# Earlier first tile, gated casts and a new order of visits in a fused attention and MLP kernel

## The chip, the cores and the metric

The kernel runs on one core of a Trainium2 chip. Times are device microseconds of one execution. The time before was 373.53 us, the median of 4 runs (372.5 to 373.75). The profiled run of the kernel before is a fifth one, and it took 374.65 us. The profiled executions had a mean granted TensorE clock of 0.993 to 1.000. The "span" is the time from the first to the last instruction in the profile; it is about 2 us shorter than the device time.

## The reference, cut to what matters

```python
# q, k, v: [8, 12, 448, 64] float32; w_in: [768, 2048]; w_out: [2048, 768]
scores = q @ k.T / sqrt(64) - log(448)        # per batch and head
attn   = 1 / (1 + exp(-scores))               # a sigmoid, no softmax
x      = (attn @ v), heads side by side       # [3584, 768]
h      = x @ w_in
out    = (h * sigmoid(h)) @ w_out             # [3584, 768] float32
```

Below, FF1 is the product with w_in and FF2 the product with w_out. A "bank" is a part of PSUM, the memory that TensorE writes to, and an "eviction" is the copy out of it.

## The kernel before: the parts that matter

A batch is three quads of four heads. TensorE runs through everything in one fixed order: attention of the next batch (the "visits", each of one to three units, a unit being a score step with its sigmoid, or the value product of a quad) is woven into the MLP of the batch before it. FF1 of batch 0 is 96 plain matmuls; later FF1 and FF2 stages multiply sums of blocks, and VectorE makes those sums.

The head: VectorE and ScalarE warm up, k of quad 0 comes as float32 and is cast by VectorE, everything else of the first two batches comes by GpSimd's casting loads (DMAs that turn float32 into float16 on the way).

```python
nc.vector.memset(bias_s, NEG_LOG_S)
nc.scalar.activation(warm[:, 0:1], bias_s, AF.Sigmoid, bias=bias_s, scale=1.0)
nc.vector.memset(warm, 0.0)               # waits for the activation
...
load32(1, 0)                              # k, quad 0, two DMAs on one queue
load16(0, 0)                              # q, quad 0, casting load by GpSimd
make_identity(nc, ident)
...                                       # VectorE casts k in two parts
load16(1, 1); load16(0, 1); load16(1, 2); load16(0, 2); load16(2, 0)
dummy(12)                                 # warm TensorE up on zeros
... # transposes of quad 0, then the first scores
behind = [
    [L(1, 3), L(0, 3), T(1, 1, 2)],       # loads of quad 3, transposes of quad 1
    ...
    [T(0, 2, 3), L(1, 5), L(0, 5), L(2, 2), W(0), W(1)],   # w_in pieces 0 and 1
    [], [T(1, 3, 2)], [T(0, 3, 3)],       # transposes of quad 3
    ...
    [V(2, 2, 3, 4), F(4)],                # first 4 matmuls of FF1, batch 0
```

Later quads are fetched as float32 and cast by GpSimd, then transposed by DMA:

```python
def prepare(i):
    for t in (1, 0):
        cast(t, i)                        # GpSimd, into st16[t]
        dma_transpose(t, i)
for i in range(NQ + 1, B * NQ - 2):
    at(("s", i, 3), lambda j=i + 2: prepare(j))
```

The end of a FF2 stage on VectorE is: eviction of the last value product to xT, four subtractions of 0.27 us (`x_sums`), the last two evictions of FF2, then sums of gT for the next FF2 (`g_sums`).

## Time and profile before

| | before |
|---|---|
| time, median of 4 | 373.53 us |
| span of the profiled run (374.65 us) | 372.9 us |
| TensorE busy, idle | 358.4 us, 14.5 us |
| first score | 9.18 us |
| first FF1 matmul of batch 0 | 29.70 us |
| FF1 of batch 1, 2, 3 starts | 60.75, 107.95, 153.04 us |

The rows from "first score" down are starts of TensorE's instructions in the timeline. The difference between two of them is the length of a stage. The prediction below shows the lines themselves.

### The profile page before, as it was taken

To read this page: it belongs to the slowest core of one execution; us is meant where nothing else is said; L and a number is where in the kernel's file an instruction comes from. 1 tells how busy PE (TensorE), PEld (TensorE's weight loads), DVE (VectorE), ACT (ScalarE), POOL (GpSimd) and SP (SyncE) were. 2 spreads that over 40 slices of the span, in tenths; PEclk is the share of its full clock that TensorE was granted. 3 is DMA by queue.
4 is the path that set the end of the run, shared out by engine and by line. 5 is a ranking of instruction groups with operands and counts; after the bars stand their busy time and mean duration, and the time that the engine had idled before them with its cause. 6 is when DMAs were issued, how large, how long until landed. Compare 5 with 4: busy or idle time off the path is not lost.

```text
span 372.9 us, 8674 instructions
## 1 busy us (share of the span) xinstructions
PE 358.4 (96%) x3598; PEld 238.9 (64%) x3598; DVE 229.9 (62%) x385; ACT 255.0 (68%) x290; POOL 161.1 (43%) x162
## 2 busy tenths in 40 slices
PE   6988999999999999999999999999999999999995
PEld 2553446964469755796548955598447965489652
DVE  2762698859775665755746656527368657436762
ACT  2998885777746788467884688657994679846100
POOL 8962230394322933249222691228733491006500
PEclk9999999999999999999999999999999999999999
DMA  8999999759889099760997629964697925130133
GB/s 145 183 185 205 229 227 178 125 121 140 154 191 205 2 148 202 165 179 9 180 200 139 164 46 192 190 152 114 76 191 152 195 44 115 38 86 3 42 86 84
DMA packets 64071, 51.13 MB, mean 137 GB/s; under 512 B 36768, under 2 KB 60576, under 8 KB 64032
## 3 DMA queue, kind: packets, MB, share of 16 engines
q1 hardware_dynamic: 48464, 35.86, 44.7%
q0 software_dynamic: 15328, 14.32, 25.6%
q8 instruction: 28, 0.46, 0.5%
q10 hardware_dynamic: 240, 0.39, 0.3%
q14 instruction: 11, 0.09, 0.1%
HBM read 45.61 MB, written 11.01 MB: 152 GB/s over the span
## 4 chain that ended last, share of the span: by engine, by line
PE 82%; DVE 7%; ACT 5%; DMA 3%; issue 1%; POOL 1%; ACTq 0%; DVEq 0%
PE ffp L465 34%; PE att L343 23%; PE att L172 8%; PE att L188 7%; PE ffp L343 7%; ACT attnT L178 4%; DMA w_in_sb<-in_moe_w_in_dram 3%; PE ffp L87 1%; DVE xT L206 1%; DVE w_out_sb L424 1%; DVE xT L218 1%; PE att L275 1%; PE ffp L275 1%; DVE sw L311 1%; DVE sw L310 1%
## 5 line engine op out<-in xcount | busy, mean ns | idle before, releaser
L178 ACT ACTIVATE attnT<-att,bias_s 128x896 f16<-128x896 f32 x168 | 156.8, 1013 | 26.7 <-PE att L172 23.6
L364 POOL TENSOR_TENSOR gT<-attnT,gT 128x896 f16<-128x896 f32 x42 | 77.9, 1885 | 65.5 <-ACT gT L362 65.5
L126 POOL CAST st<-st 128x896 f16<-128x896 f32 x36 | 35.0, 987 | 107.9 <-DMA st<-in_k_dram 95.3
L343 PEld LDWEIGHTS <-w_in_sb 128*128 128x128 f16 x672 | 64.4, 98 | 1.8 <-issue 1.1
L374 ACT COPY attnT<-att 128x896 f32<-128x896 f32 x35 | 31.7, 905 | 45.9 <-PE att L343 45.9
L343 PE MATMUL att<-xT,w_in_sb 128*128 128x224 f16 x588 | 61.1, 259 | 0.5 <-DVE xT L206 0.5
L465 PEld LDWEIGHTS <-gT 128*128 128x128 f16 x416 | 39.3, 98 | 29.2 <-issue 5.6
L465 PEld LDWEIGHTS <-gs 128*128 128x128 f16 x384 | 34.7, 98 | 31.9 <-issue 11.7
L465 PE MATMUL ffp<-w_out_sb,gT 128*128 128x384 f16 x288 | 51.3, 326 | 0.0
L343 PEld LDWEIGHTS <-sw 128*128 128x128 f16 x504 | 48.3, 98 | 1.4 <-issue 1.4
L362 ACT ACTIVATE gT<-attnT 128x896 f16<-128x896 f32 x42 | 39.9, 951 | 11.7 <-DVE attnT L378 10.9
L172 PE MATMUL att<-qkT,qkT 64*64 64x448 f16 x588 | 42.0, 359 | 2.6 <-ACT attnT L178 1.0
L378 DVE TENSOR_TENSOR attnT<-att,attnT 128x896 f32<-128x896 f32 x28 | 30.6, 1091 | 21.4 <-PE att L343 19.9
L206 DVE TENSOR_SCALAR xT<-att 128x896 f16<-128x896 f32 x22 | 24.0, 1090 | 27.6 <-PE att L188 24.5
L465 PE MATMUL ffp<-wt,gs 128*128 128x384 f16 x192 | 36.3, 327 | 0.0
L465 PE MATMUL ffp<-w_out_sb,gs 128*128 128x384 f16 x192 | 36.1, 327 | 0.0
L476 DVE TENSOR_SCALAR snap<-ffp 128x384 f32<-128x384 f32 x40 | 22.2, 554 | 22.3 <-PE ffp L465 22.2
L343 PE MATMUL att<-xT,sw 128*128 128x224 f16 x336 | 35.6, 259 | 0.0
L188 PE MATMUL att<-attnT,v 64*64 64x448 f16 x588 | 32.8, 352 | 0.0
L172 PEld LDWEIGHTS <-qkT 64*64 64x64 f16 x588 | 17.3, 105 | 24.2 <-issue 17.6
L479 DVE SCALAR_TENSOR_TENSOR osb<-ffp,snap 128x384 f32<-128x384 f32 x40 | 22.1, 554 | 15.3 <-PE ffp L465 15.0
L378 DVE TENSOR_TENSOR attnT<-ffp,attnT 128x448 f32<-128x448 f32 x28 | 16.1, 616 | 19.7 <-PE ffp L343 19.7
(71 smaller groups left out, 343.6 us busy)
## 6 DMA issues: line engine op xcount, KB each, us to landing
out_dram<-osb SPq DMA_DIRECT2D x53, 192.0 KB, 3.1
st<-in_k_dram SPq DMA_DIRECT2D x38, 224.0 KB, 4.5
st<-in_q_dram SPq DMA_DIRECT2D x36, 224.0 KB, 4.9
v<-in_v_dram POOLq DMA_DIRECT2D x44, 112.0 KB, 4.3
w_in_sb<-in_moe_w_in_dram POOLq DMA_DIRECT2D x4, 768.0 KB, 14.9
w_out_sb<-in_moe_w_out_dram POOLq DMA_DIRECT2D x4, 768.0 KB, 20.2
sw<-in_k_dram POOLq DMA_DIRECT2D x8, 112.0 KB, 4.5
sw<-in_q_dram POOLq DMA_DIRECT2D x8, 112.0 KB, 4.6
```

The lines of the kernel that those rows point to most:

```text
L126: nc.gpsimd.tensor_copy(st16[kind].rearrange("p r e d -> p e r d"), st32[kind].rearrange("p e (r d) -> p e r d", r=R),)
L172: nc.tensor.matmul(att[pair][cj, e, :S], kT[re, r, cj], qT[re, :, cj], start=True, stop=True)
L178: nc.scalar.activation(attnT[:, s0 : s0 + 2, :], att[pair][:, :, :S], AF.Sigmoid, bias=bias_s, scale=QKSCALE)
L188: nc.tensor.matmul(bank(pair, j)[e * HP : (e + 1) * HP, :S], vt[rj, e, r, :], attnT[rj, s0 + e, :], start=(r == 0), stop=(r == R - 1),)
L206: nc.vector.tensor_scalar_mul(x, att[pair][:, :, :S], SX)
L343: nc.tensor.matmul(o, a[:, c, (4 * s + f) * P : (4 * s + f + 1) * P], xb[:, c], start=first and c == 0 and f % 2 == 0, stop=c == KC - 1, s ...
L362: nc.scalar.activation(oo, ap, AF.Sigmoid, bias=0.0, scale=ISX)
L364: nc.gpsimd.tensor_mul(oo, ap, oo)
L374: nc.scalar.copy(as2(h[:, i, c], ap), ap)
L378: nc.vector.tensor_add(as2(h[:, i, c], ap), ap, as2(h[:, i, c], ap))
L465: nc.tensor.matmul(bank, a[:, fc], w[:, fc], start=first and fc == 0, stop=fc == KH - 1, skip_group_check=True,)
L476: nc.vector.tensor_scalar_mul(snap[i], bank, ISX)
```

## The change

Its intent: start TensorE's warm-up and the first scores earlier; keep GpSimd's casts apart in time from the sums that VectorE makes on the way to the next FF1; and place the visits of batch 1 better between the FF1 steps of batch 0.

```diff
+    nc.vector.memset(warm, 0.0)
     nc.vector.memset(bias_s, NEG_LOG_S)
-    nc.scalar.activation(warm[:, 0:1], bias_s, AF.Sigmoid, bias=bias_s, scale=1.0)
-    nc.vector.memset(warm, 0.0)
...
-    load32(1, 0)
+    for lo, hi in ((0, 4), (4, R)):
+        c = slice(lo * D, hi * D)
+        for g, queue in enumerate((nc.sync, nc.scalar)):
+            queue.dma_start(st32[1][g * HP : (g + 1) * HP, :, c], src_of(1, 0, g)[:, :, c])
     load16(0, 0)
+    nc.scalar.activation(start_s, bias_s, AF.Sigmoid, bias=bias_s, scale=1.0)
...
-    dummy(12)
+    dummy(10)
...
-        (8, "v", 0), (17, "v", 0), (26, "v", 0), (32, "w", 0), (35, "v", 0), ...
+        (8, "v", 0), (21, "v", 0), (24, "w", 0), (30, "v", 0), (35, "v", 0), ...
...
-        at(("s", i, 3), lambda j=i + 2: prepare(j))
+        if i % NQ < NQ - 1:
+            at(("s", i, 3), lambda j=i + 2: prepare(j))
...
         if parts[0][1] == 2:
             g_sums(parts[0][0], 4)
+        if b + 1 < B:
+            for t in range(2):
+                nc.vector.memset(st16[t][:, 0, 0, 0:1], 0.0)
+            prepare(b * NQ + NQ + 1)
         ff1(b, ((1, 3), (2, 0)))
```

Below, "the head" is the first part of this, "the new order" the list of visits, and "the gate" the memsets with the moved `prepare`: the cast must wait for a one-element write that stands behind the sums in VectorE's order.

## The prediction

> **What bounds the kernel now.** I read the page first, then the list of waits, then the timelines of the three places that the change touches. The page says that TensorE is the bound almost everywhere:
> ```profile
> PE 358.4 (96%) x3598; PEld 238.9 (64%) x3598; DVE 229.9 (62%) x385; ACT 255.0 (68%) x290; POOL 161.1 (43%) x162
> ```
> The reader is to see how little there is to win: the span is 372.9 us, so TensorE idles 14.5 us in all. 2% is 7.5 us. The table of stretches of 10 us puts the idle time in few places: 3.3 us in the first 10 us, 1.1 and 1.9 us in the next two, about 0.5 to 0.7 us each in the stretches from 50, 60, 80, 100 and 150 us, and 4.5 us at the end, which the change does not touch. The waits say what ended those gaps:
> ```profile
> PE ffp L275 <- DMA w_in_sb<-in_moe_w_in_dram: 1.1, 1, 1.1
> PE ffp L343 <- DVE osb L529: 1.1, 2, 0.6
> ```
> The first is a wait for the first piece of w_in at 29.7 us, the second two equal waits of 0.56 us at the starts of the second and third FF1 stage (109.8 and 154.9 us). Now the head, TensorE alone:
> ```profile
> 2.77 4.96 PE L87 MATMUL ffp<-warm 128*128 128x512 f16 x12 [2.77 <-DVE warm L80]
> 7.67 0.41 PE L148 MATMUL att<-ident,st 128*64 128x128 f16 x8
> 7.91 0.56 PE L148 MATMUL ffp<-ident,st 128*64 128x128 f16 x14
> 8.30 0.33 PE L148 MATMUL att<-ident,st 128*64 128x128 f16 x6
> 9.18 0.38 PE L172 MATMUL att<-qkT,qkT 64*64 64x448 f16 x4 [0.55 <-ACT qkT L158]
> ```
> Twelve dummies start late (VectorE's memset of `warm` waited for ScalarE's warm-up activation, which writes a column of it) and end at 7.7 us, although the k tile was in and cast before that; VectorE's own timeline has its cast behind the last landing of k:
> ```profile
> 6.53 0.69 DVE L569 CAST st<-st 128x512 f16<-128x512 f32 x2 [3.81 <-DMA st<-in_k_dram]
> ```
> So the head looks like 1 to 2 us of free gain. But GpSimd issues the casting loads of the next quads back to back, each pair in about 1.2 us, from 1.25 us until w_in:
> ```profile
> 9.08 1.25 POOL L119 DMA_DIRECT2D st<-in_k_dram  x2
> 10.32 1.20 POOL L119 DMA_DIRECT2D st<-in_q_dram  x2
> ```
> These are k and q of quad 3. The DMA views of 5 to 10 us and of 10 to 15 us give their time to landing (last column, us):
> ```profile
> st<-in_k_dram POOLq DMA_DIRECT2D x2, 112.0 KB, 4.6
> ```
> ```profile
> st<-in_q_dram POOLq DMA_DIRECT2D x2, 112.0 KB, 4.5
> ```
> The second DMA of each pair is issued half a pair later, so quad 3's k is complete at 9.08 + 0.62 + 4.6 = 14.3 us and its q at 10.32 + 0.60 + 4.5 = 15.4 us. TensorE uses them here:
> ```profile
> 14.62 0.58 PE L148 MATMUL att<-ident,st 128*64 128x128 f16 x14
> 15.20 0.38 PE L172 MATMUL att<-qkT,qkT 64*64 64x448 f16 x4
> 15.52 0.58 PE L148 MATMUL ffp<-ident,st 128*64 128x128 f16 x14
> ```
> So the kernel runs only 0.3 and 0.1 us behind its loads at 15 us. And the chain that ended last does not go through the dummies after that; it goes through GpSimd's issues and this load:
> ```profile
> 19.19 10.46 DMA w_in_sb<-in_moe_w_in_dram
> ```
> The first w_in piece lands at 29.65 us, and FF1 of batch 0 cannot start before, whatever ScalarE and TensorE have finished. DMA is 9 tenths busy from the first landing to 70 us.
>
> The third place is the end of a batch's last visits, all engines:
> ```profile
> 107.65 0.27 DVE L218 TENSOR_TENSOR xT<-xT 128x224 f16<-128x224 f16 x1
> 107.66 1.05 POOL L126 CAST st<-st 128x896 f16<-128x896 f32 x1 [7.04 <-DMA st<-in_k_dram]
> ...
> 107.83 1.00 DVE L218 TENSOR_TENSOR xT<-xT,xT 128x224 f16<-128x224 f16 x1
> ```
> The same subtraction takes 0.27 us alone and 1.00 us when GpSimd's cast of the prefetched k tile runs. What follows on VectorE (the last two evictions of FF2, L479 and L529) ends 0.73 us later, and TensorE waits 0.56 us for the bank that L529 frees. The next sum (L446) also goes from 0.69 to 1.35 us under the cast of q, but nothing waits for it then.
>
> **What the skill says.** The Trainium skill, "SBUF — State Buffer", section "Who interferes with whom": a VectorE instruction with two SBUF inputs contends with a GpSimd instruction that reads SBUF, and the one that starts first blocks the other until it is done. The trace agrees: the sum at 107.83 us ends just after the cast (108.71 us), and the 0.73 us added is most of one cast. "DMA: Bandwidth & Descriptors", section "Issuing engines are not separate DMA queues": several issuing engines save only the sequencer's issue time, since all DMAs share the same 16 engines. Here the two k issues took 1.43 us on one queue, so the saving can be about 0.7 us. "TensorE: Matmul & The Clock Gate", section "What's actually happening": the array runs at half clock until it has been busy for some 3.4 us. The trace shows dummies starting 0.43 us apart until about 7 us and 0.2 us for the last two, so ten dummies should warm it up, or nearly.
>
> **The change, part by part.**
>
> *Head.* Removed: the wait of `warm` for the activation (1.6 us) and two dummies. The memset comes first on VectorE, at about 0.8 us for 0.27 us, so the dummies start at about 1.15 us and ten of them at 0.43 us end at 5.4 us in place of 7.7 us. k in four parts on two queues: the first parts of both halves are issued at 0.73 us together; before, the first issued DMA had the 4.2 us median to landing, and 256 KB now come where 224 KB came, so they should be in at about 4.5 to 5 us, the rest at about 6. ScalarE has the table load and its activation behind two issues, done near 4 us, before it is wanted. The q tile still comes by GpSimd, issued at 1.25 and 1.9 us with a similar 4.1 us or more in a busy stretch, so at about 6.1 to 6.7 us; its transposes and the two copies (0.35 and 0.3 us) give a first score at about 7.7 us in place of 9.18: **1.5 us earlier**. On the path to the end: almost none. Scores stay ahead only until the transposes of quad 3, which cannot move before 14.3 and 15.4 us; there 0.1 to 0.3 us of the 1.5 are left. What is left runs into w_in at 29.65 us: GpSimd's order is unchanged, its only idle time before the issue is 0.21 us (L119 at 11.73 us), so w_in lands at most 0.2 us earlier. I book **0.1 us**.
>
> *Gated casts.* The memsets of one element of `st16` stand in VectorE's order behind the x sums (and the g sums where FF2 starts with a pair), the casts behind them. Added: two memsets of about 0.06 us for each of six batches, beside TensorE. Moved: casts and DMA transposes some 1 to 4 us later, into a FF1 stage of about 15 us; the tiles are first scored some 10 us after that stage, so nothing should wait for them. Removed: 0.56 us at the second and 0.56 us at the third FF1 stage, the two waits listed: **1.1 us**. The other FF1 starts show no wait. The cast under the long sum of w_out at 84 us (3.88 us for two, 1.82 elsewhere; then 0.71 us of TensorE waiting) belongs to a quad whose prepare is not moved, so that wait stays.
>
> *Visits of batch 1 moved.* The same work in another order between 30 and 62 us. TensorE's visible waits there are 0.32 us (56.0), 0.35 us (59.3) and 0.54 us (62.2); and score groups of eight that take 0.49 us when fed are stretched to about 0.8 us at 36.7 and 39.3 and 0.7 us at 46.9: about 0.8 us. Sum: some 2 us at most. ScalarE is almost as full (8.9 of 10 us from 30 to 50). The new order has 13 steps before the second visit, which takes away the stretch at 36.7, spreads the w sums out, and takes the long in-place sum out of the way of the last eviction to xT. Against it: visits only 5 and 4 steps (1.0 and 0.8 us) apart, where two sigmoids need 1.9 us, and two steps between the last two visits. I book **0.4 us**.
>
> Sum: 0.1 + 1.1 + 0.4 = 1.6 us; 373.5 - 1.6 = **371.9 us**.
>
> **Rivals.** (a) The head counts in full: 1.5 us more, 370.4 us. For it: the dummies stand on the chain. Against it: loads at 14.3, 15.4 and 29.65 us that do not move. It would need w_in to land earlier. (b) The casts merely hit other VectorE work in FF1, or the late transposes hold up a score: the 1.1 us are lost or halved, about 372.6 us. Against it: VectorE has idle stretches there, and its work on PSUM has only one SBUF input. (c) The new order of visits is worse: ScalarE piles up between the close visits and TensorE loses 0.5 to 1 us, giving about 373 us. (d) The new order takes most of its 2 us: 370.3 us.
>
> **Range and chances.** Each term has about its own size as its error: head 0 to 0.7 (1.5 in the rival), casts 0.5 to 1.4, order -0.7 to 1.5. Combined, 0.2 to 3.2 us, and the runs before spread over 1.1 us. Range 370.3 to 373.3 us. Over 2% would need 7.5 us, half of all idle time; slower by 2% would need a new wait in every batch. Faster 0.02, same 0.97, slower 0.01.
>
> **What would show each step.** Right: first score near 7.7 us, but the quad 3 transposes at 14.3 and 15.4 us or later, a wait for w_in grown to about 2 us, FF1 of batch 0 still starting at 29.4 to 29.8 us; no L218 of 1.00 us, no waits of L343 for L529; the 0.71 us wait near 88 us still there. Wrong: FF1 of batch 0 starting over 0.7 us earlier, a wait of a score for a transposed tile, or TensorE idling more from 30 to 62 us than its 1.4 us of before.

## The result, and the profile after

The changed kernel took 374.87 us (median of 4, 374.31 to 375.48) against 373.53 us for the kernel before. The ratio is 1.0042, with a 95% interval of 1.0017 to 1.0066. Ratios are the mean time of one kernel's fast runs over that of the other's of the same rounds, so they are not quite the ratio of the medians; nor quite that of the means over all rounds that I quote below, from which they differ by up to 0.0010. Later rounds, told below, put the same two kernels at 0.9990 to 0.9998.

The page of the changed kernel has almost the same TensorE line; busy time says nothing here:

```profile
PE 358.9 (96%) x3596; PEld 239.2 (64%) x3596; DVE 224.0 (60%) x397; ACT 255.6 (69%) x290; POOL 160.0 (43%) x162
```

The list of TensorE's waits (total us, times, longest us) does say something:

```profile
PE ffp L148 <- DMA st<-in_q_dram: 2.5, 2, 2.0
PE att L172 <- ACT attnT L178: 1.7, 5, 0.5
PE ffp L87 <- DVE bias_s L80: 1.2, 1, 1.2
```

The waits for w_in (1.1 us) and for the evicted bank (1.1 us in two) are gone from the list. In their place stands one wait of 2.0 us for a q tile. TensorE's timeline of the head shows it (start us, us busy, then the wait in brackets):

```profile
1.19 4.45 PE L87 MATMUL ffp<-warm 128*128 128x512 f16 x10 [1.19 <-DVE bias_s L80]
5.57 0.64 PE L148 MATMUL att<-ident,st 128*64 128x128 f16 x8
6.62 0.83 PE L148 MATMUL ffp<-ident,st 128*64 128x128 f16 x14 [0.42 <-DMA st<-in_q_dram]
...
8.14 0.38 PE L172 MATMUL att<-qkT,qkT 64*64 64x448 f16 x4 [0.52 <-DVE qkT L158]
...
14.31 0.58 PE L148 MATMUL att<-ident,st 128*64 128x128 f16 x14 [0.17 <-DMA st<-in_k_dram]
...
17.24 0.83 PE L148 MATMUL ffp<-ident,st 128*64 128x128 f16 x14 [2.03 <-DMA st<-in_q_dram]
...
30.73 0.93 PE L275 MATMUL ffp<-xT,w_in_sb 128*128 128x448 f16 x4
```

The first score comes 1.04 us earlier than before. At 14.31 us, k of quad 3 leaves 0.3 us of that. Then q of quad 3, used at 15.52 us before, holds TensorE until 17.24 us. FF1 of batch 0 starts at 30.73 us, 1.03 us later than before, and this time it waits for no w_in.

The third reading is the end of the second FF2 stage:

```profile
108.70 0.27 DVE L218 TENSOR_TENSOR xT<-xT,xT 128x224 f16<-128x224 f16 x1
...
109.36 0.55 DVE L529 TENSOR_SCALAR osb<-ffp 128x384 f32<-128x384 f32 x1
...
109.97 1.31 PE L343 MATMUL ffp<-xT,sw 128*128 128x224 f16 x12
...
112.39 0.07 DVE L709 MEMSET st<- 128x1 f16 x2
...
112.60 1.81 POOL L126 CAST st<-st 128x896 f16<-128x896 f32 x2 [11.72 <-DVE st L709]
```

The fourth sum takes 0.27 us in place of 1.00, the second product of FF1 (109.97 us) waits for nothing, and the casts run behind the memsets. The stage from FF1 of batch 2 to FF1 of batch 3 is 44.38 us (108.82 to 153.20) in place of 45.09. So one part did what it should, and something else gave more back.

### The profile page after: what moved, and what is told of

Same layout as the page of the kernel before. It is cut to its first block, busy times and chain, and to the rows that moved or that the text cites. A ratio compares the mean times of both kernels' runs of the same rounds, so it can differ in the third digit from the quotient of the medians.

```text
span 373.1 us, 8705 instructions
## 1 busy us (share of the span) xinstructions
PE 358.9 (96%) x3596; PEld 239.2 (64%) x3596; DVE 224.0 (60%) x397; ACT 255.6 (69%) x290; POOL 160.0 (43%) x162
## 5 line engine op out<-in xcount | busy, mean ns | idle before, releaser
L126 POOL CAST st<-st 128x896 f16<-128x896 f32 x36 | 34.1, 967 | 118.6 <-DMA st<-in_k_dram 52.0
L362 ACT ACTIVATE gT<-attnT 128x896 f16<-128x896 f32 x42 | 39.9, 951 | 11.6 <-DVE attnT L378 10.9
L188 PE MATMUL att<-attnT,v 64*64 64x448 f16 x588 | 33.7, 359 | 0.0
```

The lines of the kernel that those rows point to most:

```text
L126: nc.gpsimd.tensor_copy(st16[kind].rearrange("p r e d -> p e r d"), st32[kind].rearrange("p e (r d) -> p e r d", r=R),)
L188: nc.tensor.matmul(bank(pair, j)[e * HP : (e + 1) * HP, :S], vt[rj, e, r, :], attnT[rj, s0 + e, :], start=(r == 0), stop=(r == R - 1),)
L362: nc.scalar.activation(oo, ap, AF.Sigmoid, bias=0.0, scale=ISX)
```

## The experiments

Each was run with five rounds (six runs, profiled one included) unless said otherwise. Rounds ran in four sessions: chip 2, chip 0 twice (these two share eleven runs of the kernel before), chip 9.

### First session: one part at a time

**The kernel before against itself.** No edit.

> The kernel before, unchanged, against itself: ratio 1.000 with an interval of some 0.2%. It also gives a second trace. If the loss of the change is real, its trace again has no wait of TensorE for the q tile of quad 3 (about 15.4 us), FF1 of batch 1 starting at 60 to 61 us, and the span is below the changed kernel's by the 0.3% or so that the times differ by. If instead the first profile of before was a lucky or unlucky sample, the start of FF1 of batch 1 moves by 1 us or more between the two traces of the same kernel.

Measured: 374.55 us mean (373.14 to 376.67), ratio 0.9999, interval 0.9965 to 1.0033. The seventeen runs of the kernel before on this chip spread from 372.73 to 376.67 us. The three timed runs that I had before the prediction spread over 1.1 us; with the profiled run (374.65 us), which I also had and left out, it is 2.15 us. So a single kernel moves by 4 us from one execution to the next, and one trace shows one draw. In its second trace FF1 of batch 1 started at 60.88 us (60.75 in the first), q of quad 3 was transposed at 16.45 us in place of 15.52, and only one of the two waits for the bank was there.

**The head alone.**

```diff
 # the memset, load, activation and dummy(10) hunks of the change; nothing else
```

> Before plus the head part alone (early memset, k in four parts on two queues, late table warm-up, ten dummies). Theory A, the head does the harm: TensorE runs early into the loads of quad 3, sits over 1 us on them, its clock is granted at less than full afterwards (the changed kernel's trace has 2.03 us and a granted clock of 0.87 from 10 to 20 us), and the time is 1.5 to 2.5 us above before (ratio 1.004 to 1.007). Theory B, the order of visits does it: the head alone is within 0.3 us of before (ratio 0.999 to 1.001) or a little faster.

Measured: 375.08 us mean against 374.52, ratio 1.0013, interval 0.9985 to 1.0041: no gain, and no loss that stands clear of the spread. Its list of waits:

```profile
PE ffp L465 <- DVE snap L476: 1.8, 1, 1.8
PE ffp L275 <- DMA w_in_sb<-in_moe_w_in_dram: 1.5, 1, 1.5
```

The first score came at 7.71 us, 1.5 us earlier than in the first trace of before, and FF1 of batch 0 waited 1.5 us for w_in and started at 29.94 us. That is the head's gain ending in a wait for a load. Theory A and theory B both fall as put: neither part costs 1.5 us by itself. The wait of 1.8 us is at 88 us, in a part that the change does not touch.

**The gate alone.**

```diff
 # the two hunks with prepare and the memsets of st16
```

> Before plus the gated casts alone. My step of the prediction: 1.1 us less (ratio 0.997), no VectorE sum of 1.00 us, no wait of FF1 for the eviction of the bank before its second product at the second and third stage. If the gain is given back in some other wait, the ratio is 0.999 or more.

Measured: 373.79 us mean against 374.52 (-0.73 us), ratio 0.9984, interval 0.9946 to 1.0022, so the times alone do not tell the gain from zero. One of the six runs took 376.7 us; the other five lie between 372.85 and 373.42. No wait for the bank in the trace, nor in any of the twelve traces with the gate; the two stages are 44.37 and 44.38 us. The gain is smaller than my 1.1 us, for a reason that the traces of all kernels without the gate show together: the waits for the bank at the second and third FF1 numbered 2, 1, 1 and 0 in the traces of before, before again, head and new order. The cast starts when its DMA lands, and that is sometimes on top of the sums and sometimes not.

**The new order alone.**

```diff
 # PROGRAM replaced by that of the change; nothing else
```

> Before plus the new order of visits alone. Theory A (the head does the harm): within 0.7 us of before either way (ratio 0.998 to 1.002). Theory B (the order does it): 1.5 to 2.5 us slower (1.004 to 1.007), with waits of scores for sigmoids near 40 us and of the last values for the last sigmoid near 60 us, together over 1.2 us.

Measured: 374.34 us mean against 374.52, ratio 0.9993, interval 0.9963 to 1.0024. The waits that I had named against it are there:

```profile
PE att L172 <- ACT attnT L178: 1.9, 6, 0.5
...
PE ffp L465 <- DVE snap L476: 0.9, 1, 0.9
PE att L188 <- ACT attnT L178: 0.7, 1, 0.7
```

Scores wait for sigmoids near 39 and 40 us, and the last values wait 0.7 us. From the first FF1 matmul of batch 0 to FF1 of batch 1 it takes 31.18 us (29.44 to 60.62), as in all other traces with the new order to within 0.01 us. With the old order, this stage takes 30.97 to 31.14 us in the five traces of before, before again, head, gate, and both gates below (later 30.97 and 31.11 us; the two traces with head, moved loads and the old order have 31.31 and 35.95 us, for losses told of there). So the new order costs 0.04 to 0.2 us there, and wins nothing by itself.

### Second session: the whole again, the whole without its head, and two theories on where gains go

**The changed kernel again.** No edit.

> The changed kernel again, on one chip with the others. The first rounds made it 0.4% slower than before; but before against itself now spreads over 3 us. If the loss is real: ratio 1.003 to 1.006 again. If it came from that session: ratio 0.997 to 1.001, and its trace lacks the 2.03 us wait for quad 3's q[...].

Measured: 373.74 us mean against 374.21, ratio 0.9990, interval 0.9974 to 1.0006. FF1 of batch 1 started at 60.07 us in place of 61.91, since q of quad 3 came at 16.05 us.

**The changed kernel without its head.**

```diff
 # the gate and the new order on the old head
```

> The changed kernel with its head part undone (gated casts and the new visits on the old head). If the head does the harm, this is 0.5 to 2 us faster than the changed kernel in the same rounds, and about 0.7 us faster than before (ratio 0.997 to 0.999). If the head does nothing, the two are equal within 0.3 us.

Measured: 373.44 us mean against 374.21, ratio 0.9982, interval 0.9965 to 0.9999. It is 0.3 us faster than the changed kernel of the same rounds; the spans differ by 0.2 us in the mean, which the spread does not tell from zero. Its trace has a wait of 1.33 us for q of quad 3, with the old head. So that wait is not made by the head.

**Both gates.** While reading the traces I saw the same collision at 84 us, at casts that the change leaves alone, and worse: a long sum of w_out takes 3.88 us for two instructions; later sums of the same size take 1.82. These are the lines of before (start us, us, engine, what):

```profile
84.23 3.88 DVE L424 TENSOR_TENSOR w_out_sb<-w_out_sb 128x1536 f16<-128x1536 f16 x2
...
85.47 1.82 POOL L126 CAST st<-st 128x896 f16<-128x896 f32 x2
...
88.63 1.30 PE L465 MATMUL ffp<-wt,gT 128*128 128x384 f16 x7 [0.71 <-DVE snap L476]
```

```diff
 # the gate of the change, and for quad 8, which is prepared at 84 us:
-at(("s", i, 3), lambda j=i + 2: prepare(j))
+at(("s", i, 3), lambda j=i + 2: (gate16() if j == 2 * NQ + 2 else None, prepare(j)))
 # gate16 is the same two one-element memsets of st16
```

> Before plus the gated casts of the change, plus the same gate (two one-element memsets on VectorE) ahead of the casts of the quad prepared at 84 us, where the long sum of w_out takes 3.9 us in place of 1.8 and TensorE waits 0 to 1.8 us in the six traces at hand. If the shared port is the cause there too: no wait of FF2 for the snap copy near 88 us, the stage from the first to the second FF1 of whole batches 46.5 us in place of 46.5 to 48.3, and about 0.8 us less on average than the gated casts alone. If it is not the port, the wait stays.

Measured: 372.39 us mean against 374.21 (-1.82 us), ratio 0.9954, interval 0.9936 to 0.9972. Its timeline:

```profile
83.86 2.29 DVE L424 TENSOR_TENSOR w_out_sb<-w_out_sb 128x1536 f16<-128x1536 f16 x2
...
86.11 0.07 DVE L555 MEMSET st<- 128x1 f16 x2
86.32 1.80 POOL L126 CAST st<-st 128x896 f16<-128x896 f32 x2 [0.66 <-issue]
...
87.38 1.30 PE L465 MATMUL ffp<-wt,gT 128*128 128x384 f16 x7
```

The wait is gone. FF1 of batch 1 to FF1 of batch 2 takes 46.33 us (60.38 to 106.71), where the nine traces of other kernels up to then have 46.47 to 48.32 us (the shortest of them had no wait at 88 us by luck). So two small gates on one mechanism are worth more than the whole change.

**The head with its way cleared.**

```diff
 # the head, and:
-    load16(2, 0)                                   # v of quad 0, before quad 3
-    [L(1, 3), L(0, 3), T(1, 1, 2)],
+    [L(1, 3), L(0, 3), L(2, 0), T(1, 1, 2)],
-    ... L(2, 2), W(0), W(1)],
+    ... L(2, 2), <first half of W(0)>, <second half of W(0)>, W(1)],
```

> The head part alone, with two loads moved so that its gain can pass: the first w_in piece in two halves (the first FF1 of batch 0 needs only the first half), and v of quad 0 loaded behind k and q of quad 3. My account (the gain of the head is swallowed by quad 3's q and by w_in): quad 3's transposes run near 13.3 and 14.3 us, FF1 of batch 0 starts at 27.5 to 28.5 us in place of 29.2 to 29.9, FF1 of batch 1 starts at 59 to 59.8 us in place of 60.2 to 60.9, time about 1 us below before. If the gain is lost elsewhere, FF1 of batch 1 still starts at 60.2 us or later.

Measured: 374.34 us mean against 374.21, ratio 1.0011, interval 0.9980 to 1.0041. Its timeline of TensorE has what I expected:

```profile
14.76 0.58 PE L148 MATMUL ffp<-ident,st 128*64 128x128 f16 x14
...
27.74 0.93 PE L275 MATMUL ffp<-xT,w_in_sb 128*128 128x448 f16 x4
```

q of quad 3 no longer waits, FF1 of batch 0 starts at 27.74 us and FF1 of batch 1 at 59.05 us, 1.2 to 2.6 us ahead of the traces with the old head so far (60.21 to 61.61 us). So in this trace the head's gain passes where the loads of quad 3 and w_in had swallowed it. How much they swallow varies: in the four traces of the changed kernel, told above and below, FF1 of batch 0 starts at 28.27 to 30.73 us with the unmoved loads. Which of the two moves counts was not tested. The time is nevertheless no better. This trace lost 1.41 us at 86 us and 0.56 us at 152 us, both times to casts on top of sums, and 0.66 us at 49 us to a gate product behind stretched sums of w_in; and two of the six runs took 375.5 and 376.5 us.

### Third session: a third look, everything together, and a side question

**The changed kernel a third time.** No edit.

> The changed kernel a third time. Two sessions gave +0.4% and -0.1% against before. My account now (gated casts -0.7 us, head about +0.15 us outside the span of instructions and nothing inside, visits 0, and a spread of about 1 us from one execution to the next of either kernel): ratio 0.997 to 1.0005, about -0.5 us. If the first session was right about the kernel, 1.002 to 1.006.

Measured: 373.83 us mean against 374.18, ratio 0.9993, interval 0.9975 to 1.0011. As my account had it.

**Both gates, the head and the moved loads**, old order of visits. The edits are those above, together.

> Gated casts of the change, the second gate at 84 us, the head, the two moved loads (first w_in piece in halves, v of quad 0 behind quad 3); the old order of visits. If the gains add up (1.8 us of the two gates, some 1.2 us of the head once its way is free): 2.5 to 3 us below before, ratio 0.992 to 0.9935, FF1 of batch 1 starting near 59 us and FF1 of batch 2 near 105.4 us. If the head's gain is lost again later: ratio 0.995 as with the two gates alone.

Measured: ratio 0.9957, interval 0.9919 to 0.9995. Four runs took 371.4 to 372.0 us, one 376.0 and one 378.1. The last, being over 1.5% above the fastest, is left out of the ratio; the mean of the five others is 372.51 us against 374.18. Its clock (0.995) is that of the others, so it may as well be one more run with the loss shown next; with it the mean is 373.44 us. The profiled one is the run of 376.0. Its waits begin with the first line here; VectorE's timeline has the second:

```profile
PE ffp L275 <- DVE gT L290: 3.3, 1, 3.3
```

```profile
47.16 0.56 DVE L310 TENSOR_TENSOR sw<-w_in_sb 128x768 f16<-128x768 f16 x1 [2.45 <-DMA w_in_sb<-in_moe_w_in_dram]
47.76 1.64 DVE L311 TENSOR_TENSOR sw<-sw,w_in_sb 128x768 f16<-128x768 f16 x1
49.43 1.18 DVE L312 TENSOR_TENSOR sw<-w_in_sb,sw 128x768 f16<-128x768 f16 x1
```

VectorE sits 2.45 us in front of a sum that needs the last w_in piece, two sums are then stretched by casts, and TensorE waits 3.3 us for the gate product that stands behind them; from 52 to 57 us its granted clock is then 0.66. A TensorE that is early does not bring the load of w_in forward; VectorE meets it in its own order.

**The same without head and moved v**, so two gates and the first w_in piece in halves.

> The same without the head and without the moved v: two gates and the w_in piece in halves. The wait for w_in (0 to 1.1 us in the traces with the old head) goes, so 1.8 to 2.6 us below before (0.993 to 0.995), FF1 of batch 0 starting at 28.6 to 29 us. The difference to the run with the head is what the head is worth when it can pass: 0.5 to 1 us.

Measured: 371.92 us mean (371.37 to 372.80) against 374.18 (-2.26 us), ratio 0.9941, interval 0.9924 to 0.9959. It has the lowest mean, though not clear of the last two kernels below (372.16 and 372.19 us, on another chip), and beats both kernels. The start of FF1 of batch 0 was not as expected in the one trace: 30.28 us, since q of quad 3 was 1.37 us late. So the trace does not show what the halves of w_in are worth; the mean of six runs lies 0.5 us below that of both gates without them, from other rounds on the same chip.

**The head on one queue** (three rounds, four runs).

```diff
-        for g, queue in enumerate((nc.sync, nc.scalar)):
+        for g, queue in enumerate((nc.sync, nc.sync)):
```

> The head alone, but all four parts of k on the SyncE queue, none on ScalarE's. In the kernels with the head the time is 1.94 to 2.03 us above the span of instructions, in those without it 1.78 to 1.81. If the early use of ScalarE's DMA queue makes that, it is 1.8 here; if the earlier start of the program's work makes it, 1.95. First score later than with two queues: about 8.5 us against 7.7 to 8.1.

Measured: 374.49 us mean against 374.18, ratio 0.9998, interval 0.9976 to 1.0020. The time above the span is 1.81 us in the mean. All kernels with the two-queue head have 1.92 to 2.07 us, all with the old head 1.78 to 1.82. So the use of ScalarE's queue for a first load goes with about 0.15 us that no instruction of the profile shows. The first score came at 8.23 us.

### Fourth session: what was still open

**The changed kernel a fourth time.** No edit.

> The changed kernel a fourth time. My account: 0.998 to 1.0005 of before. If the first session's loss belongs to the kernel on some chips: 1.002 or more on one of the chips.

Measured: 373.84 us mean against 374.23, ratio 0.9998, interval 0.9972 to 1.0025 (its means and its medians, 373.51 and 373.97 us, both differ by 0.1%).

**The changed kernel plus the second gate.**

```diff
+# gate16() ahead of prepare(8), as above
```

> The changed kernel plus the gate ahead of the casts at 84 us. The gate alone took about 1.1 us off; here its trace had waits of 0.4, 1.1 and 0.65 us there, so 0.7 to 1.1 us below the changed kernel, ratio to before 0.996 to 0.998, and no wait near 88 us.

Measured: 372.93 us mean against 374.23, ratio 0.9968, interval 0.9951 to 0.9986; 0.91 us below the changed kernel of the same rounds, with no wait near 88 us. Not all of that need be the wait: a loss of 0.35 us near 320 us, told of under "Why the prediction was wrong", is in the changed kernel's traces and not in this one.

**The changed kernel plus second gate and moved loads.**

> The changed kernel plus second gate, w_in's first piece in halves, v of quad 0 behind quad 3. If the new order of visits is what makes the early head safe: no runs at 376 us and more, about 371.2 us, ratio 0.991 to 0.993, FF1 of batch 1 near 59 us. If the order does nothing for it: again one run in three or so at 375 us or more, with VectorE waiting for w_in near 45 us or TensorE for VectorE near 49 us.

Measured: 372.16 us mean (371.65 to 372.94) against 374.23, ratio 0.9948, interval 0.9932 to 0.9964. FF1 of batch 1 starts at 58.92 us, the earliest of all. None of six runs took over 373 us, where the two kernels with early head, moved loads and old order had four of twelve at 375.5 us or more. That fits the account that the new order, which moves the two groups of sums that need the last w_in piece from steps 54 and 64 to 77 and 67, makes the early head safe; twelve and six runs do not prove it.

**The same without head and moved v.**

> The same without the head and without the moved v. If the head is worth something once its way is free: 0.5 to 1.2 us above the run with the head. If not: equal to it, about 371.9 us as with the old order of visits.

Measured: 372.19 us mean against 374.23, ratio 0.9949, interval 0.9930 to 0.9967. Equal to the kernel with the head. I had expected 0.5 to 1.2 us. In the mean the span is 0.2 us longer and the time above the span 0.2 us shorter. The profiled trace with the head has lost 0.41 us again at 86 us, where the earlier VectorE meets GpSimd's gate products in place of the casts.

The kept traces show one more place where the head loses, the end of the program. From the end of the last eviction (L529) to the end of the span it takes 4.17 to 4.26 us in all ten traces with the head, that of one queue included, and 3.80 to 3.86 us in all eight without. SyncE's wait for the last stores shows it (the changed kernel again, then the same without its head):

```profile
SPq L754 <- DMA out_dram<-osb: 2.3, 1, 2.3
SPq L750 <- DMA out_dram<-osb: 1.9, 2, 1.2
```

Among the semaphore instructions of the traces, SyncE's last waits stand in a row, about 0.06 us apart when nothing holds them. In the traces looked at, seven still follow the wait for the last store with the head (head alone, one queue, the changed kernel, and with second gate and moved loads), one with the old head. That the head's two additional loads shift this order is likely, but no run tests it. With the 0.15 us outside the span, about 0.5 us of what the head wins by 60 us is so lost again. The rest is not found: the one trace without the head is of its slowest run (373.61 us).

## Why the prediction was wrong

I predicted 371.9 us, from 370.3 to 373.3. The rounds gave 374.87 us. Three later sessions gave 373.74, 373.83 and 373.84 us (means), 0.4 us below before each time, so even the more favourable number is outside my range and a quarter of the gain that I forecast. In short, no part was worth what I booked for it: the gate's waits were counted as present in every execution (1.1 us booked, about 0.75 measured), the head has costs behind the loads that I had not looked for (+0.1 booked, about -0.3 measured, with a spread of that size), and the new order had the wrong sign (+0.4 booked, 0.04 to 0.2 us lost). Step by step:

**The head, booked at 0.1 us.** Its mechanism was right: the first score at 7.67 to 8.14 us in the nine traces of the head with two queues, as worked out; the gain gone at quad 3's loads and at w_in; and with those moved, FF1 of batch 0 at 27.74 us. Five things failed. First, "the transposes of quad 3, which cannot move before 14.3 and 15.4 us" took a landing that had been read once as fixed. q of quad 3 was waited for or not, by up to 2.03 us, with either head. The same holds for "w_in lands at most 0.2 us earlier" than 29.65 us: in the fourth trace of the changed kernel FF1 of batch 0 started at 28.27 us, with no wait for w_in. Second, such a wait can bring a lower granted clock with it: the second row below is the changed kernel from 17 to 21 us (us, PE, PEld, DVE, ACT and POOL busy, then granted clock), and the same 0.57 stands in five other traces, four that waited 1.33 to 1.54 us and that of before again, which waited 0.89 us.

```profile
10.00:17.00 7.00, 4.42 (x78) 2.22 (x72) 4.83 (x9) 6.08 (x7) 5.76 (x10) 1.00 1.22 185
17.00:21.00 4.00, 3.76 (x50) 2.16 (x54) 1.16 (x2) 2.14 (x3) 3.61 (x6) 0.57 1.11 160
```

Third, 0.15 us outside the span, which I had not thought of. Fourth, the 0.37 us at the end of the program, told above. Fifth, in the changed kernel itself, the way from FF1 of batch 6 to FF1 of batch 7 takes 44.68 us in all four traces, and 44.32 to 44.33 us in the fourteen traces of other kernels: an eviction to xT near 320 us waits 2.14 us, for the scores that follow its value product, in place of 1.79 us for the product. The head, the gate or the order alone do not show it, nor does the change without its head; its cause is open. The head is worth about zero or a little less than zero: 0.3 us slower than no head in the same rounds.

**The gate, booked at 1.1 us.** The mechanism was right, the size was off. "The two waits listed" were both present in one trace, but they are a draw: in the six traces of ungated kernels (before, before again, head, new order, head with moved loads, head on one queue) I count 2, 1, 1, 0, 1 and 2. That is 1.17 in the mean, times 0.71 us for each (45.09 less 44.38 us; the wait that the list shows, 0.56 us, is not all that is lost), so 0.83 us; measured were 0.73 us for the gate alone and 0.77 us for the kernel without head, which has the new order too.

**The new order, booked at 0.4 us.** Wrong in sign. My rival (c) is what happened, at a smaller size: the close visits cost 0.73 us in two waits near 39 us, the last values 0.69 us in place of 0.35, and the stage became 0.04 to 0.2 us longer.

**The wait at 88 us, "so that wait stays".** Right that it stays, and it was the largest thing in reach: I read 0.71 us of it; over the traces it is 0 to 1.83 us, and adding the second gate to the changed kernel, which took it away, was worth 0.9 us.

**The range.** "The runs before spread over 1.1 us" came from three runs, without the profiled one at 374.65 us. Seventeen runs on one chip spread over 3.9 us. I had combined errors of the terms, and hardly anything for the draw.

**What stays open.** Why the first rounds had the change 0.4% above before. Its profiled run lost 2.0 us at q of quad 3, so FF1 of batch 1 started at 61.91 us, 1.5 to 2.5 us later than in the three later traces of the same kernel. That accounts for that one run. The other three of those rounds have no trace, and before was at 373.3 us in the mean there, 0.9 to 1.2 us under its later means; the fifth run of that time, the profiled one, took 374.65 us. A chip on which the two really differ, or four runs of each that fell badly, cannot be told apart. Nor is it known what makes q of quad 3 late; in the changed kernel's first trace an instruction fetch of 16 KB took 1.9 us at that moment (1.0 us before), but in four other traces with waits over 1.3 us it took 0.9 to 1.2 us.

## What to carry to other kernels

Before booking a wait of half a microsecond as a gain, find out whether it is in every execution: a second and third trace of the kernel before cost little and would have shown these waits as draws. When one collision is found (here GpSimd's cast of one SBUF tile under VectorE's sums of two), look for every place of its kind; the place that the change left alone was worth more than the one it mended. Work that starts earlier only helps as far as the next load that does not move, and a load that another in-order engine waits for can be hit even earlier than before. Loads added at the start can also cost after the last product, so compare the ends of two traces too.

## What the Trainium skill lacked or had wrong

- "SBUF — State Buffer", section "Who interferes with whom", held: a VectorE sum of two SBUF inputs took 1.00 us in place of 0.27 under a GpSimd cast, and gates that keep them apart gained 1.8 us of 374.2. The page does not say that the loss varies between executions of one kernel when the cast starts at a DMA's landing: 0 to 2 such waits here for one gate's places, 0 to 1.83 us at the other.
- "TensorE: Matmul & The Clock Gate", section "What's actually happening", has the clock at half speed after at least one idle window of about 3.4 us. Half speed and a length of 3.41 us are what the clock records of the traces show. But the window need not be idle: in the 3.41 us before the seven drops inside the kernels TensorE was busy 0.40 to 1.99 us. In all other stretches of 3.41 us, counted from the clock's rise in each of the eighteen traces up to 366 us, it was busy 1.91 us or more. So the limit lies near 1.9 to 2.0 us (an estimate from the profile's busy times, which are modelled). That section gives none.
- "DMA: Bandwidth & Descriptors", section "Issuing engines are not separate DMA queues", says that more issuing engines save only the sequencer's time. The saving shows faintly (first score at 7.7 to 8.1 us in nine traces with two queues, 8.23 us in the one with one). No page has the cost: 1.92 to 2.07 us of device time above the span of instructions with a first load on ScalarE's queue, 1.81 us in the same head without. Nor does a page have the 0.37 us that the head's two more loads go with at the end of the program (3.80 to 3.86 us after the last eviction without the head, 4.17 to 4.26 us with it).
- No page gives a spread of landing times: the two 112 KB loads of q of quad 3, issued by GpSimd from 10.2 to 10.9 us in the traces with the old order of loads, took 4.3 to 5.7 us to land (median of the two) and made TensorE wait 0 to 2.03 us.
